# A mixture-of-experts kernel: the second and third expert run in two row tiles of 64, a chunk's two pieces of 272 tokens side by side

## The chip, the cores and the metric

One core of a Trainium2 chip runs the whole program. The metric is the device time of one execution in microseconds, the median over runs. The core has engines that work side by side, each through its own list of instructions in order, and wait for one another by semaphores: TensorE (PE: matrix products into PSUM banks; its loads of the stationary operand are listed as PEld), VectorE (DVE), ScalarE (ACT), GpSimd (POOL) and SyncE (SP, which here issues most of the DMAs).

## The reference

Linear attention (16 heads of 28) and a mixture of 8 experts with two chosen per token run on the same 2048 x 448 input, and a gate per token mixes them. The change is in the experts:

```python
logits = xf @ w_gate
topk_idx = jnp.argsort(-logits, axis=-1)[:, :K]          # K = 2
gates = _softmax(jnp.take_along_axis(logits, topk_idx, axis=-1), axis=-1)
for e in range(E):                                       # E = 8
    mask = (topk_idx == e)
    w = (gates * mask).sum(-1, keepdims=True)
    h = _silu(xf @ w1[e]) @ w2[e]                        # 448 -> 1792 -> 448
    out = out + w * h
...
return g * a + (1 - g) * b
```

## The kernel before

The attention part and the routing come first, and then the experts, ordered by how many tokens chose them, the fullest first. Experts are named 0 to 7 here. Each has room for a fixed number of tokens (`ROOMS`: 552, 544, 544, 504, 504, 504, 496, 488); a loop at the end takes what is above it. The first three (`LARGE` = 3) have more than 512, so `extra(e)` is 40, 32 and 32 tokens; the extras of 32 are called narrow.

Every float32 operand is split into a rounded part (names ending in h) and the rest (names ending in l), and a product is made of three: high by high, high by low, low by high.

**First layer.** The 1792 hidden units of an expert are worked in 14 chunks of 128 (`fc`). For a chunk the weights w1 stand in the array and the tokens stream past. The depth of 448 is three blocks of 128 and one of 64. Experts 0 to 2 use the whole array (`first`, products in `mm3` at L144): the tokens go in two pieces of half the room (276 or 272 columns), one after the other, and a piece takes 11 products: 8 for the high part of the tokens, with the 64 rows that the last block leaves free used for a low part, and 3 for the low part. Experts 3 to 7 use the array as two row tiles of 64 rows (`first_pair`, `in_halves`, L1038): a round is two products of 64 rows that run side by side, one in each half of the array, for two chunks with all tokens (504, 496 or 488 columns). Depth 448 is seven half blocks of 64, three products each: 21 rounds for the two chunks. The first 12 rounds have chunk 0 in the lower half and chunk 1 in the upper, and the last 9 have them the other way round.

**Between the layers.** `gated` takes a sum from its PSUM bank: ACT applies Silu (L1071), DVE makes the high part (a cast, L1077) and the low part (a subtraction, L1080), and for narrow experts copies the extra tokens' columns (L1075). The sums have the two banks "A", used in turn.

**Second layer.** For a chunk, four blocks of 128 tokens (`c` = 0 to 3; `c` = 4 is expert 0's extra tokens) are multiplied with w2 and added up over the 14 chunks: 12 products of 448 columns a chunk, 14 in expert 0. Experts 0 to 2 do it with the whole array (`second`, `share`, L1156), experts 3 to 7 in row tiles for two chunks at a time (`second_pair`, L1122: 24 rounds, blocks 0 and 1 in one half while 2 and 3 are in the other, then exchanged). The narrow extra tokens are multiplied at the end of an expert in `side_by_side` (L1138). Sums of blocks 2 and 3 lie in one double bank, the others in four banks "O". At an expert's end `leave` scales each sum by the token's gate: even blocks by DVE (L1181), odd ones by ACT (L1179), and POOL scatters the rows.

**Order of the work.** The order on each engine is that of the code. A loop over the 112 chunks prepares the next weights (`halve`: ACT copies, DVE subtracts), the next expert's tokens (`gathers` asks for them, `tokens` turns and splits them), and then does its products. For experts 0 to 2 a finished chunk is put into `held`, and its second layer comes one or two chunks later; only expert 2's last two go through the queue. For experts 3 to 7 a generator `queue` runs through second-layer pairs round by round, and `go_on(n)` takes n rounds from it; the pair's first layer is 12 rounds, then 12 of the queue, the other 9, and 12 of the queue. When a bank's sum passes from one half of the array to the other, `meet` places a wait: SP waits for the earlier product, and TensorE waits for SP.

Of the kernel before, what the change touches and what calls it, by code (L numbers as in the profile page):

```python
# [83 lines left out]
SPLITS = {0: (7, 8), 1: (9, 10), 2: (11,), 3: (12,), 4: (13,), 5: (14,), 6: (15,)}  # L84
FILL = ((0, 0), (0, 1))
APART = 24


@with_exitstack
def gated_mix(ctx: ExitStack, tc: tile.TileContext, xt, xq, wk, wq, wv, wphi, wo, w12, out):  # L90
# [15 lines left out]
    def bank(tag, name):  # L106
        pool, n = banks[tag]
        return pool.tile([P, 512], F32, tag=tag, name=name, bufs=n)
# [693 lines left out]
    def extra(e):  # L802
        return EXS[e] if e < LARGE else 0
# [5 lines left out]
    def narrow(e):  # L809
        return 0 < extra(e) <= 32  # L810
# [45 lines left out]
    def tokens(e, c):  # L856
        if c == 0:
            pool = pf if e % 2 else pw
            xg[e] = (pool.tile([P, 4, CAP], F32R, tag="xgh", name=f"xgh{e}", bufs=1),
                     pool.tile([P, 4, MAIN] if e >= LARGE else [P, 3, CAP], F32R, tag="xgl", name=f"xgl{e}", bufs=1))  # L860
        xgh, xgl = xg[e]
        if (e, c) not in xg:
            return
        t = xg[e, c]
        n, m = (4, P) if c < nm else (-(-extra(e) // 32), extra(e))
        xt_ = pm.tile([P, 4, P], F32, tag="xt", name=f"xgt{e}{c}")
        for b in range(n):
            nc.vector.transpose(xt_[:, :, b * 32:(b + 1) * 32], t[:, b].rearrange("p (c k) -> p c k", c=4))
        yield
        m = min(m, ROOMS[e] - c * P)  # L870
        at = slice(c * P, c * P + m)
        both(xgh[:, :, at], xgl[:, :, at], xt_[:, :, 0:m], e >= LARGE)


    def first_tokens(c):
# [147 lines left out]
        beats.append(i)  # L1023
        reached["pe"] = i

    def in_halves(o, xh, xl, wh, wl):
        rounds = []
        for own, turned_ in (((0, 1, 2, 3), False), ((0, 1, 2), True)):
            for s in own:
                for w, x in ((wh, xh), (wl, xh), (wh, xl)):  # L1030
                    one = [(1 - a if turned_ else a, a) for a in range(2)]
                    rounds.append([(i, a, w[half[a], s, i * P:(i + 1) * P], x[half[a], s])
                                   for i, a in (reversed(one) if turned_ else one)])
        for n, one in enumerate(rounds):
            if n == 12:
                yield
            for i, a, l, r in one:
                meet(("first", i), a, lambda: nc.tensor.matmul(o[i], l, r, start=n == 0, stop=n == len(rounds) - 1),  # L1038
                     n == 0)

    def first_pair(e, pair):
        n = ROOMS[e]
        xgh, xgl = (x[:, :, 0:n] for x in xg[e])
        hp = [bank("A", f"hp{e}_{2 * pair + i}")[:, 0:n] for i in range(2)]
        yield from in_halves(hp, xgh, xgl, *wts[e * (NFC // 2) + pair, 1])
        for i in range(2):
            gated(e, 2 * pair + i, 0, hp[i])

    def first(e, fc, hf):
        s, i = divmod(e * NFC + fc, 2)  # L1050
# [34 lines left out]


    def accs(e):
        own = [nm, 0, 1] if extra(e) else [0, 1] if e + 1 < E else range(nm)
        a = {c: bank("O", f"acc{e}{c}") for c in own}
        if e + 1 == E:  # L1090
            return a
        pair = two_banks(f"acc{e}").rearrange("p j n -> p (j n)")
        for i in range(2):
            a[2 + i] = pair[:, i * 512:(i + 1) * 512]
        return a
# [13 lines left out]
    def second_pair(e, pair):  # L1109
# [3 lines left out]
        if narrow(e) and ends:  # L1113
            for at in range(0, NFC, BATCH):
                side_by_side(e, range(at, min(at + BATCH, NFC)))
        todo = [(c, l, r) for c in range(nm) for i in range(2) for l, r in products(e, 2 * pair + i, c)]
        n = len(todo) // 2
        todo = [(a, *one) for k in range(2 * n) for a, one in enumerate((todo[k], todo[k - n]))]
        of = [one[1] for one in todo]
# [4 lines left out]
            if k % 2 and k + 1 < len(todo):  # L1124
                yield
        if ends:
            leave(e, (2, 3, *order(e)[:-2]))
            if e == E - 2:
                settle()
        yield  # L1130
# [66 lines left out]
    def order(e):  # L1197
        return (*([nm] if extra(e) else []), *range(nm))
# [15 lines left out]
    for t in range(NT + 2):  # L1214
# [67 lines left out]
        if SPLIT <= t < SPLIT + 3 and splits:  # L1282
            if next(splits[0], 0) == 0:
                del splits[0]
                if splits:
# [9 lines left out]
    pf = pf_stack.enter_context(tc.tile_pool(name="pf", bufs=2, reuse_waits="tile"))  # L1295
    load(1)
    held = []
    queue = (h for e, pair in [(LARGE - 1, NFC // 2 - 1), *((e, pair) for e in range(LARGE, E)
                               for pair in range((NFC - LATE * (e == E - 1)) // 2))] for h in second_pair(e, pair))

    def go_on(n):
# [4 lines left out]
    for s in range(E * NFC):  # L1306
        e, fc = divmod(s, NFC)
        k, i = divmod(s, 2)
        token = tokens(e + 1, fc - 9) if e + 1 < E and 9 <= fc <= 9 + nm else iter(())
        next(token, 0)  # L1310
        if i == 0 and k + 2 < E * NFC // 2:
            load(k + 2)
# [4 lines left out]
        if e + 1 < E and fc == 4:  # L1317
            asked = gathers(e + 1)
        if e + 1 < E and fc >= 4:
            for _ in range(2):  # L1320
                next(asked, None)
        if e < LARGE:
            for hf in range(2):
                if (e, fc, hf) not in fill:
                    first(e, fc, hf)
            held.append((e, fc))
            advance(1)
            while len(held) > (1 if e == 0 or fc == 0 else 2):
                h = held.pop(0)
                second(*h)  # L1330
                if h[1] == NFC - 1:
                    leave(h[0], order(h[0]))
            continue
        advance(1)
        n = 3 * nm
        if e == E - 1 and fc > NFC - LATE:
            n = n // 2 if fc < NFC - 1 else 0
        if fc % 2 == 0:
            f = first_pair(e, fc // 2)
            next(f)  # L1340
            go_on(n)
            next(f, None)
        else:
            go_on(n)
# [114 lines left out]
```

## Time and profile before

| | |
|---|---|
| time, median of 3 runs | 792.2 us (791.98 to 792.21) |
| the profiled execution | 792.33 us, of which the span from the first to the last instruction is 790.5 us |
| instructions in the profile | 18467 |
| granted TensorE clock, mean | 0.993 of full |
| TensorE products | busy 777.1 us, 98% of the span, 7542 |
| TensorE weight loads | 718.6 us, 91%, 7542 |
| VectorE | 481.6 us, 61% |
| ScalarE | 309.3 us, 39% |
| GpSimd | 336.8 us, 43% |
| DMA | 85.95 MB, 109 GB/s on average |

The profile is one execution, and its times are counted from the start of the span. Products are pipelined, so a row's length is longer than the distance from one start to the next; distances between starts tell how fast TensorE goes on. A wait is put down to the engine or transfer that ended it last; "issue" stands for idle time that ends without anything the profile shows.

### The profile page before, as it was taken

What the parts mean: (1) busy time and instruction counts of PE and PEld (TensorE: products, weight loads), DVE (VectorE), ACT (ScalarE), POOL (GpSimd) and SP (SyncE); (2) the same over time, 40 slices, a digit from 0 to 9 for tenths busy, and PEclk for the clock granted to TensorE, in tenths of its full rate; (3) what the DMA queues carried; (4) which work ended last, traced back from release to release, by engine and by line L of the source; (5) the groups of instructions that cost most, each with busy time, mean ns of one, the idle gap of its engine ahead of it and who ended that gap; (6) DMA issues with size and microseconds to landing.
All of it is one profiled execution on the core that took longest, in us unless ns stands there. A gap on an engine that the chain in (4) does not pass through costs nothing.

```text
span 790.5 us, 18467 instructions
## 1 busy us (share of the span) xinstructions
PE 777.1 (98%) x7542; PEld 718.6 (91%) x7542; DVE 481.6 (61%) x1045; ACT 309.3 (39%) x522; POOL 336.8 (43%) x318
## 2 busy tenths in 40 slices
PE   9999999999999999999999998999999999999995
PEld 6888888888999999998998897999999999999994
DVE  4798978778775865675574543554744555475431
ACT  5543455666533443333242322332433333243221
POOL 5667877875132235414540445144325405423003
PEclk9999999999999999999999998999999999999998
DMA  8420000153433346317541552364345336434403
GB/s 274 126 86 1 2 3 26 34 125 124 140 124 124 118 83 191 102 63 158 146 134 51 126 144 87 107 153 130 122 120 152 134 118 160 140 126 110 137 2 47
DMA packets 39789, 85.95 MB, mean 109 GB/s; under 512 B 11313, under 2 KB 20929, under 8 KB 39701
## 3 DMA queue, kind: packets, MB, share of 16 engines
q1 hardware_dynamic: 29332, 67.88, 26.2%
q0 software_dynamic: 10224, 16.61, 11.3%
q8 instruction: 61, 1.00, 0.6%
q10 hardware_dynamic: 144, 0.23, 0.1%
q14 instruction: 28, 0.22, 0.1%
HBM read 71.89 MB, written 12.82 MB: 107 GB/s over the span
## 4 chain that ended last, share of the span: by engine, by line
PE 84%; issue 10%; DVE 3%; POOL 1%; ACT 1%; POOLq 0%; DVEq 0%; ACTq 0%
PE acc L1122 16%; PE hp L1038 16%; PE hp L144 15%; PE acc L1156 13%; PE ao L144 5%; PE pk L144 4%; PE pq L658 3%; PE pv L144 2%; PE n L909 2%; PE pv L355 2%; PE early L658 1%; PE et L729 1%; PE kv L637 1%; POOL out_dram L994 1%; PE acc L1138 1%
## 5 line engine op out<-in xcount | busy, mean ns | idle before, releaser
L1122 PE MATMUL acc<-w2h,hx 64*128 64x448 f32 (+3 forms) x1088 | 194.3, 366 | 0.1
L828 POOL DMA_INDIRECT xg<-in_xq_dram,idq x114 | 127.4, 1118 | 155.0 <-PE hp L1038 57.1
L1071 ACT ACTIVATE hs<-hp 128x272 f32<-128x272 f32 (+4 forms) x154 | 70.8, 483 | 312.9 <-issue 179.4
L1077 DVE CAST hx<-hs 128x504 fp32r<-128x504 f32 (+5 forms) x154 | 55.6, 361 | 208.0 <-ACT hs L1071 201.0
L1122 PEld LDWEIGHTS acc<-w2h,hx 64*128 64x128 f32 (+3 forms) x1088 | 162.5, 184 | 5.6 <-ACT y L1179 1.6
L1122 PE MATMUL acc<-w2l,hx 64*128 64x448 f32 (+3 forms) x544 | 155.7, 366 | 0.0
L1038 PE MATMUL hp<-xgh,w1h 64*128 64x504 f32 (+2 forms) x490 | 146.3, 387 | 1.2 <-issue 1.2
L1038 PE MATMUL hp<-xgh,w1l 64*128 64x504 f32 (+2 forms) x490 | 145.9, 386 | 0.6 <-issue 0.6
L1038 PE MATMUL hp<-xgl,w1h 64*128 64x504 f32 (+2 forms) x490 | 145.6, 385 | 0.9 <-issue 0.9
L994 POOL DMA_INDIRECT out_dram<-y,tabm x32 | 52.2, 1631 | 172.4 <-DVE y L1181 164.0
L1156 PE MATMUL acc<-w2h,hx 128*128 128x448 f32 (+2 forms) x366 | 111.7, 365 | 0.0
L1122 PEld LDWEIGHTS acc<-w2l,hx 64*128 64x128 f32 (+3 forms) x544 | 97.7, 184 | 1.4
L1038 PEld LDWEIGHTS hp<-xgh,w1h 64*128 64x128 f32 x490 | 88.0, 185 | 5.5 <-issue 2.8
L1038 PEld LDWEIGHTS hp<-xgh,w1l 64*128 64x128 f32 x490 | 87.9, 185 | 4.0 <-issue 1.2
L1038 PEld LDWEIGHTS hp<-xgl,w1h 64*128 64x128 f32 x490 | 88.0, 185 | 3.2 <-issue 0.5
L1080 DVE TENSOR_TENSOR hx<-hs,hx 128x276 fp32r<-128x276 f32 (+5 forms) x168 | 84.9, 512 | 5.3
L144 PE MATMUL hp<-xgh,w1h 128*128 128x272 f32 (+1 forms) x336 | 87.9, 289 | 0.0
L144 PE MATMUL hp<-xgh,w1l 128*128 128x272 f32 (+1 forms) x336 | 87.8, 289 | 0.0
L797 DVE TENSOR_TENSOR w1l<-wr,w1h 128x1024 fp32r<-128x1024 f32 x56 | 68.2, 1219 | 11.1 <-ACT w1h L795 9.9
L1156 PEld LDWEIGHTS acc<-w2h,hx 128*128 128x128 f32 (+2 forms) x366 | 68.0, 186 | 6.2 <-issue 0.7
L1156 PE MATMUL acc<-w2l,hx 128*128 128x448 f32 (+2 forms) x190 | 69.4, 365 | 0.0
L144 PEld LDWEIGHTS hp<-xgh,w1l 128*128 128x128 f32 x336 | 63.2, 188 | 0.6
(236 smaller groups left out, 1393.5 us busy)
## 6 DMA issues: line engine op xcount, KB each, us to landing
wr<-in_w_dram SPq DMA_DIRECT2D x56, 512.0 KB
wr<-in_w_dram SPq DMA_DIRECT2D x46, 448.0 KB
kept<-in_w_dram SPq DMA_DIRECT2D x10, 448.0 KB
out_dram<-aos SPq DMA_DIRECT2D x16, 224.0 KB
xr<-in_xt_dram SPq DMA_DIRECT2D x10, 256.0 KB
xg<-in_xq_dram,idq POOLq DMA_INDIRECT x114
xr<-in_xt_dram SPq DMA_DIRECT2D x6, 192.0 KB
out_dram<-zero SPq DMA_DIRECT2D x5, 224.0 KB
```

The source lines that it names most:

```text
L144: reached["pe"] = nc.tensor.matmul(o, a, b, start=i == 0, stop=i == n - 1)
L355: nc.tensor.matmul(pv2[t][:, 0:VG], a, (WL if k == "w" else WH)["v"][:, c], start=c == 0 and k == "h", stop=c == 3 and k == "w")
L658: nc.tensor.matmul(pq[t].rearrange("p h d -> p (h d)"), x, w, start=k == 0, stop=k == 10)
L797: nc.vector.tensor_tensor(out=l, in0=raws[s][layer - 1], in1=h.bitcast(F32), op=ALU.subtract)
L828: i = nc.gpsimd.indirect_dma_start(out=t[:, b], out_offset=None, in_=xq, in_offset=bass.IndirectOffsetOnAxis(ap=idq[:, e, 4 * c + b:4 * c ...
L994: return nc.gpsimd.indirect_dma_start(out=out, out_offset=bass.IndirectOffsetOnAxis(ap=idx_ap, axis=0), in_=y, in_offset=None, compute_op= ...
L1038: meet(("first", i), a, lambda: nc.tensor.matmul(o[i], l, r, start=n == 0, stop=n == len(rounds) - 1), n == 0)
L1071: nc.scalar.activation(hs[:, tsl], hp, AF.Silu)
L1077: nc.vector.tensor_copy(h[:, tsl], hs[:, tsl])
L1080: nc.vector.tensor_tensor(out=h[:, a + o:b + o], in0=hs[:, a:b], in1=h[:, a:b].bitcast(F32), op=ALU.subtract)
L1122: meet((e, c), a, lambda: nc.tensor.matmul(acc[e][c][:l.shape[1], 0:D], l[half[a]], r[half[a]], start=new, stop=ends and c not in of[k + 1 ...
L1156: i = nc.tensor.matmul(acc[e][c][:l.shape[1], 0:D], l, r, start=fc == 0 and k == 0, stop=fc == NFC - 1 and k == len(pr) - 1)
```

## The change

Experts 1 and 2 now run in row tiles too (`TILED` = 1 is the first expert that does). A round holds the same chunk for both pieces of 272 tokens, one piece in each half of the array (`first_pieces`), so a chunk takes 21 rounds of 272 columns in place of 22 products. Its rounds are 12, then `LEAD` = 5 rounds of the queue, the other 9, and the remaining 7 of the queue; in the first two chunks of expert 1 the queue gets 7 and 7, since expert 0's last pair has 28 rounds. The second layer of experts 1 and 2, and of expert 0's last two chunks, goes through `second_pair`.

Beside it: tokens of experts 1 and 2 are split into a full low part (a depth of four blocks, as in experts 3 to 7); those of expert 1 are asked for three at a time rather than two, and are turned one chunk earlier; the sums' banks are handed out in another order (`accs`), and two experts leave in another order (expert 0: blocks 4, 2, 3, 0, 1; expert 1: 2, 3, 4, 0, 1; both had 4, 0, 1, 2, 3).

```diff
+TILED = 1
+LEAD = 5
...
-    def in_halves(o, xh, xl, wh, wl):
+    def in_halves(o, ops):
         rounds = []
         for own, turned_ in (((0, 1, 2, 3), False), ((0, 1, 2), True)):
             for s in own:
-                for w, x in ((wh, xh), (wl, xh), (wh, xl)):
+                for w, x in ((2, 0), (3, 0), (2, 1)):
                     one = [(1 - a if turned_ else a, a) for a in range(2)]
-                    rounds.append([(i, a, w[half[a], s, i * P:(i + 1) * P], x[half[a], s])
+                    rounds.append([(i, a, ops[i][w][half[a], s], ops[i][x][half[a], s])
                                    for i, a in (reversed(one) if turned_ else one)])
...
+    def first_pieces(e, fc):
+        s, i = divmod(e * NFC + fc, 2)
+        w = [x[:, :, i * P:(i + 1) * P] for x in wts[s, 1]]
+        n = ROOMS[e] // 2
+        hp = [bank("A", f"hp{e}_{fc}_{hf}")[:, 0:n] for hf in range(2)]
+        yield from in_halves(hp, [(*(x[:, :, hf * n:(hf + 1) * n] for x in xg[e]), *w) for hf in range(2)])
+        for hf in range(2):
+            gated(e, fc, hf, hp[hf])
...
-        own = [nm, 0, 1] if extra(e) else [0, 1] if e + 1 < E else range(nm)
+        own = [nm, 0, 1] if e < TILED else [0, 1, nm] if extra(e) else [0, 1] if e + 1 < E else range(nm)
...
-            leave(e, (2, 3, *order(e)[:-2]))
+            leave(e, (*order(e)[-2:], *order(e)[:-2]) if e else (nm, 2, 3, 0, 1))
...
-    queue = (h for e, pair in [(LARGE - 1, NFC // 2 - 1), *((e, pair) for e in range(LARGE, E)
+    queue = (h for e, pair in [(TILED - 1, NFC // 2 - 1), *((e, pair) for e in range(TILED, E)
...
-        token = tokens(e + 1, fc - 9) if e + 1 < E and 9 <= fc <= 9 + nm else iter(())
+        at = fc - (9 if e else 8)
+        token = tokens(e + 1, at) if e + 1 < E and 0 <= at <= nm else iter(())
...
-            for _ in range(2):
+            for _ in range(2 if e else 3):
                 next(asked, None)
-        if e < LARGE:
+        if e < TILED:
...
-            while len(held) > (1 if e == 0 or fc == 0 else 2):
+            while len(held) > (1 if fc < NFC - 1 else 2):
...
-        if fc % 2 == 0:
+        if extra(e):
+            a, b = (7, 7) if (e, fc) in ((1, 0), (1, 1)) else (LEAD, n - LEAD)
+            f = first_pieces(e, fc)
+            next(f)
+            go_on(a)
+            next(f, None)
+            go_on(b)
+        elif fc % 2 == 0:
```

Three places of the order show what moves. The first is TensorE at the passage from expert 0 to expert 1 (`hp_13_1` is the second piece of expert 0's last chunk, `acc` the second layer's sums, `hp_0_0` and `hp_0_1` the pieces of expert 1's first chunk). Before, with the waits of each row in brackets, the middle products left out:

```order
L144 MATMUL hp_13_1_4426<-xgl_2995,w1h_4207 128x276 x3
L1156 MATMUL acc_3617<-w2h_4273,hx_12_4363 80x448 [waits DVE_49]
L1156 MATMUL acc_3617<-w2l_4274,hx_12_4363 80x448
L1156 MATMUL acc_3618<-w2h_4273,hx_12_4363 128x448
...
L1156 MATMUL acc_3620<-w2l_4274,hx_12_4363 128x448
L1156 MATMUL acc_3620<-w2h_4273,hx_12_4363 128x448
L144 MATMUL hp_0_0_4466<-xgh_4058,w1h_4341 128x272 [waits Activation_49]
```

Now, in the same place:

```order
L146 MATMUL hp_13_1_4421<-xgl_2995,w1h_4220 128x276 x3
L1040 MATMUL hp_0_0_4447<-xgh_4002,w1h_4344 128x272 [waits Activation_49]
L1040 MATMUL hp_0_1_4448<-xgh_4002,w1h_4344 128x272 [waits Activation_49]
L1040 MATMUL hp_0_0_4447<-xgh_4002,w1l_4345 128x272 [waits DVE_49]
L1040 MATMUL hp_0_1_4448<-xgh_4002,w1l_4345 128x272
L1040 MATMUL hp_0_0_4447<-xgl_4003,w1h_4344 128x272
```

The 14 second-layer products of chunk 12 that stood between the two experts have moved behind expert 1's first rounds, and both pieces of its first chunk begin together. The second place is DVE at expert 0's leaving, which now stands in expert 1's second chunk (`hx_1` is that chunk's split, `y_4622`, `y_4626` and `y_4632` are blocks 4, 2 and 0 of expert 0):

```order
L1092 TENSOR_TENSOR hx_1_4598<-hs_1_4597,hx_1_4598 128x272 [waits DVE_49]
L1087 COPY hxe_1_4599<-hs_1_4597 128x32 [waits Activation_49]
L1089 CAST hx_1_4598<-hs_1_4597 128x240
L1092 TENSOR_TENSOR hx_1_4598<-hs_1_4597,hx_1_4598 128x240 [waits DVE_49]
L1194 TENSOR_SCALAR y_4622<-acc_3617,tabx 80x448 [waits PE_49]
L1194 TENSOR_SCALAR y_4626<-acc_3620,tabm 128x448 [waits PE_49]
L1194 TENSOR_SCALAR y_4632<-acc_3618,tabm 128x448
L799 TENSOR_TENSOR w1l_4643<-wr_9_4439,w1h_4642 128x1024 [waits DMAHW0_49,Activation_49]
```

Before, these three stood in the order 4, 0, 2 behind the split of expert 1's first chunk; now block 2 comes ahead of 0, and all are a chunk later. The third place is TensorE in expert 1's third chunk, with the first second-layer products of that expert (`acc_4675` is the double bank of blocks 2 and 3, `acc_4672` the bank of block 0):

```order
L1040 MATMUL hp_2_0_4646<-xgl_4003,w1h_4443 128x272
L1040 MATMUL hp_2_1_4647<-xgl_4003,w1h_4443 128x272
L1135 MATMUL acc_4672<-w2h_4400,hx_0_4508 128x448 [waits DVE_49]
L1135 MATMUL acc_4675<-w2h_4400,hx_0_4508 128x448 [waits Activation_49]
L1135 MATMUL acc_4672<-w2l_4401,hx_0_4508 128x448
...
L1135 MATMUL acc_4675<-w2l_4401,hx_1_4598 128x448
L1040 MATMUL hp_2_0_4646<-xgh_4002,w1h_4443 128x272 [waits SP_sequencer_49]
L1040 MATMUL hp_2_1_4647<-xgh_4002,w1h_4443 128x272 [waits SP_sequencer_49]
```

The chunk's first 12 rounds, five rounds of the second layer, and then the exchange of halves with its wait through SP; the double bank waits for ACT.

More of the change, by code (lines that the diff above doesn't have):

```diff
@@ L859, in tokens @@
             xg[e] = (pool.tile([P, 4, CAP], F32R, tag="xgh", name=f"xgh{e}", bufs=1),
-                     pool.tile([P, 4, MAIN] if e >= LARGE else [P, 3, CAP], F32R, tag="xgl", name=f"xgl{e}", bufs=1))
+                     pool.tile([P, 4, MAIN if e >= LARGE else CAP] if e >= TILED else [P, 3, CAP], F32R, tag="xgl", name=f"xgl{e}", bufs=1))
         xgh, xgl = xg[e]
@@ L871, in tokens @@
         at = slice(c * P, c * P + m)
-        both(xgh[:, :, at], xgl[:, :, at], xt_[:, :, 0:m], e >= LARGE)
+        both(xgh[:, :, at], xgl[:, :, at], xt_[:, :, 0:m], e >= TILED)
     def first_tokens(c):
@@ L1044, in first_pair @@
         hp = [bank("A", f"hp{e}_{2 * pair + i}")[:, 0:n] for i in range(2)]
-        yield from in_halves(hp, xgh, xgl, *wts[e * (NFC // 2) + pair, 1])
+        yield from in_halves(hp, [(xgh, xgl, *(w[:, :, i * P:(i + 1) * P] for w in wts[e * (NFC // 2) + pair, 1]))
+                                  for i in range(2)])
         for i in range(2):
             gated(e, 2 * pair + i, 0, hp[i])
+    def first_pieces(e, fc):
[6 more added lines that the diff above has]
+            gated(e, fc, hf, hp[hf])
     def first(e, fc, hf):
@@ L1115, in second_pair @@
                 side_by_side(e, range(at, min(at + BATCH, NFC)))
-        todo = [(c, l, r) for c in range(nm) for i in range(2) for l, r in products(e, 2 * pair + i, c)]
+        todo = [(c, l, r) for c in (range(nm) if narrow(e) else order(e)) for i in range(2)
+                for l, r in products(e, 2 * pair + i, c)]
         n = len(todo) // 2
```

## Prediction

> **What bounds it now.** I read the page first (the chain that ended last), then who TensorE waited for, then TensorE by stage.
>
> ```profile
> PE 84%; issue 10%; DVE 3%; POOL 1%; ACT 1%; POOLq 0%; DVEq 0%; ACTq 0%
> ```
> ```profile
> PE hp L1038 <- issue: 2.7, 5, 0.9
> PE warm L241 <- DVE blank L239: 1.1, 1, 1.1
> PE n L909 <- issue: 0.6, 2, 0.4
> PE n L909 <- DVE w L925: 0.5, 1, 0.5
> ```
> ```profile
> 203.00:279.00 76.00, 76.00 (x488) 72.63 (x487) 54.21 (x165) 28.56 (x50) 18.17 (x18) 1.00 0.38 125
> 279.00:356.00 77.00, 77.00 (x509) 74.38 (x508) 49.41 (x124) 29.46 (x53) 30.44 (x23) 1.00 0.41 113
> 356.00:429.00 73.00, 73.00 (x488) 68.16 (x488) 43.86 (x105) 26.87 (x47) 30.10 (x24) 1.00 0.48 132
> ```
> The chain is TensorE; in all 790 us it waits for another engine only at the start and once for 0.5 us (columns: total, times, longest). The windows are roughly experts 0, 1 and 2 (length, then busy time of PE, weight loads, DVE, ACT, POOL): PE is busy throughout, DVE under 72%. So time here is the sum of products times their spacing, and an edit counts if it changes that sum or opens a hole in it.
>
> The spacing is read from the timeline (start, length, engine, line, names, forms, count), by starts: 12 second-layer products of expert 1 and the 22 first-layer ones of expert 2's first chunk; and, in two row tiles, 9 rounds of expert 3's first layer and 12 of its second.
>
> ```profile
> 350.56 0.36 PE L1156 MATMUL acc<-w2h,hx 128*128 128x448 f32 x1
> 352.99 0.29 PE L144 MATMUL hp<-xgh,w1h 128*128 128x272 f32 x1
> 355.75 0.36 PE L1156 MATMUL acc<-w2h,hx 128*128 128x448 f32 x1
> ```
> ```profile
> 502.08 0.56 PE L1038 MATMUL hp<-xgh,w1h 64*128 64x504 f32 x2
> 504.12 0.54 PE L1122 MATMUL acc<-w2h,hx 64*128 64x448 f32 x2
> 506.55 0.58 PE L1038 MATMUL hp<-xgh,w1h 64*128 64x504 f32 x2
> ```
> Full array: 12 products of 448 columns take 352.99 - 350.56 = 2.43, 0.2025 each; 22 of 272 take 355.75 - 352.99 = 2.76, 0.1255 each. Row tiles: 9 rounds of 504 take 2.04, 0.2267 each; 12 rounds of 448 take 2.43, 0.2025 each. The line through the two full-array points (0.0770 for 176 columns) gives 0.2270 at 504. A round of two half-height products costs what one full product of its columns costs.
>
> **The sum.** First layer: a chunk goes from 22 products to 21 rounds of 272 columns. I price the round by that line, 0.1255. Per chunk 22 x 0.1255 - 21 x 0.1255 = 0.1255; 28 chunks: **-3.5**. Second layer: 12 rounds of 0.2025 for 12 products, nothing. Expert 0's last two chunks become 28 rounds for 28 products, nothing. The narrow products of the last rows stay as they are.
>
> A round of 272 is not in this trace, and it needs two weight loads in 0.1255. Transposes of the attention part (timeline) and the page's row of expert 3's loads bound their cost:
>
> ```profile
> 170.38 0.71 PE L729 MATMUL et<-ident,eq 64*128 64x64 f32 x16
> 170.93 0.41 PE L948 MATMUL ot<-ident,om 64*128 64x64 f32 x8
> ```
> ```profile
> L1038 PEld LDWEIGHTS hp<-xgh,w1h 64*128 64x128 f32 x490 | 88.0, 185 | 5.5 <-issue 2.8
> ```
> 16 products with 16 loads of 64x128 start within 0.55: two loads and two products in 0.069, so a round of 0.1255 has room. The other end is two of the 0.185 loads one after the other, 0.37 a round, +144 over 588 rounds; the rows of 0.069 exclude it, and I take zero. [...]
>
> Instructions double in this stage: 4 in 0.1255, 32 per us, in bursts of 12 rounds, 26 over a chunk. The densest 20 us of the attention part:
>
> ```profile
> 169.00:189.00 20.00, 20.00 (x455) 17.56 (x456) 16.07 (x38) 14.51 (x25) 15.66 (x16) 1.00 0.65 193
> ```
> Here 911 were issued in 20 us, 46 per us: no cost.
>
> **New holes.** Both pieces' sums now end together, and banks are freed later or asked for sooner. Latencies come from a chunk of expert 1, in the timelines of PE (its last first-layer product starts at 308.69 + 2 x 0.1255 = 308.94), ACT and DVE:
>
> ```profile
> 308.69 0.54 PE L144 MATMUL hp<-xgl,w1h 128*128 128x272 f32 x3
> ```
> ```profile
> 307.94 0.40 ACT L1071 ACTIVATE hs<-hp 128x272 f32<-128x272 f32 x1 [2.60 <-issue]
> 309.27 0.40 ACT L1071 ACTIVATE hs<-hp 128x272 f32<-128x272 f32 x1 [0.93 <-PE hp L144]
> 309.56 1.05 ACT L795 ACTIVATE w1h<-wr 128x1024 fp32r<-128x1024 f32 x1
> ```
> ```profile
> 308.37 0.30 DVE L1077 CAST hx<-hs 128x272 fp32r<-128x272 f32 x1 [1.91 <-ACT hs L1071]
> 308.71 0.44 DVE L1080 TENSOR_TENSOR hx<-hs,hx 128x272 fp32r<-128x272 f32 x1
> 309.70 0.18 DVE L1075 COPY hxe<-hs 128x32 f32<-128x32 f32 x1 [0.55 <-ACT hs L1071]
> 309.79 0.28 DVE L1077 CAST hx<-hs 128x240 fp32r<-128x240 f32 x1
> 310.11 0.41 DVE L1080 TENSOR_TENSOR hx<-hs,hx 128x240 fp32r<-128x240 f32 x1
> ```
> And from expert 3's leaving, with expert 4's first second-layer products behind it: timelines of DVE, ACT and PE, the groups of the two y's (count, busy, mean ns) in experts 1 and 2, and the weight loads' waits.
>
> ```profile
> 517.97 1.27 DVE L1181 TENSOR_SCALAR y<-acc,tabm 128x448 f32<-128x448 f32 x2
> ```
> ```profile
> 518.68 1.16 ACT L1179 ACTIVATE y<-acc,tabm 120x448 f32<-120x448 f32 x2 [2.53 <-DVE y L1181]
> ```
> ```profile
> 518.96 0.88 PE L1122 MATMUL acc<-w2h,hx 64*128 64x448 f32 x2
> 519.37 0.67 PE L1122 MATMUL acc<-w2l,hx 64*128 64x448 f32 x2
> ```
> ```profile
> L1181 DVE TENSOR_SCALAR y<-acc,tabm 128x448 f32<-128x448 f32 x4 | 2.7, 681 | 1.6 <-PE acc L1156 1.5
> L1179 ACT ACTIVATE y<-acc,tabm 128x448 f32<-128x448 f32 x4 | 2.5, 634 | 10.0 <-PE acc L1156 7.4 <-DVE y L1181 1.3 <-issue 1.3
> ```
> ```profile
> PEld acc L1122 <- ACT y L1179: 1.6, 4, 0.5
> ```
> With T the start of a chunk's last round: Silu at T+0.33, the second 0.29 later and done at T+1.02; cast 0.43 after its Silu, subtraction 0.34 after, 0.44 long, copy, cast 0.09 later, subtraction 0.32 later, 0.41 long: DVE is through with both pieces at T+2.36. At the change from expert 3 to 4, the first second-layer product into the double bank waits for ACT's y, which waits for DVE's y (0.68 long, the next 1.27 - 0.68 = 0.59 later), which stands in DVE's queue; TensorE starts 0.06 after ACT's y (518.68 + 0.63 = 519.31, then 519.37). It loses 0.4 there, four times 1.6 in all, with 12 rounds of 504 (2.72) as cover.
>
> Hole 1, expert 0 to 1. Leaving is queued on DVE behind chunk (1, 1)'s split: y of the extra rows at T+2.36, y of token block 2 0.59 later, 0.68 long, ACT's y of block 3 0.63 long, 0.06: T+4.3. TensorE gets there at T + 0.13 + 7 x 0.2025 + 12 x 0.1255 = T+3.05. **+1.25**. Queued behind the waiting product is all of TensorE.
> Hole 2, expert 1 to 2: the same without the extra rows' y ahead, 0.6 less: **+0.65**.
> Hole 3, start of expert 1: its first round needs both banks of first-layer sums, and nothing stands between it and expert 0's last product any more (second-layer products of 2.8 us did). Silu ends at T+0.73, 0.06, against T+0.13: **+0.65**.
> Bounds for each: nothing below; 0.4 more if the tiles' halves lie 0.4 apart, as expert 3's starts do.
>
> At nothing: chunk to chunk inside an expert, banks are free at T+1.02+0.06, TensorE asks at T+0.13+1.42 = T+1.55 (cover: 7 second-layer rounds; without it 0.95 a chunk). Splits are ready at T+2.36, asked for from T+3.05 (three rounds later for the new chunk). The change of halves after round 12 waits through SP for round 12's product: 0.33 to notice and 0.06 to release, by the rows above, against 5 rounds, 1.14; SP's weight loads stand behind these waits, as in the last five experts, where TensorE's list of waits shows none for a weight. Tokens of expert 1 come one chunk earlier on DVE, which is 71% busy in that window, and change DVE's two subtractions for one. The change of tile mode moves from expert 3 to 1.
>
> Sum: -3.5 + 1.25 + 0.65 + 0.65 = -0.95. The profiled execution's own time is 792.33 (span 790.5 and 1.8 around it), so 791.4; the median of the runs is 0.13 lower, so **791.3**.
>
> **Rivals.** (a) *No holes*: if the splits of chunk (1, 1) run behind the leaving, or halves keep apart so that covers hold, -3.5: 788.8. Against: DVE takes its queue in order.
> (b) *Slower: ACT becomes late in every chunk.* ACT has a weight copy (1.05) or token copy in each chunk beside the two Silus. If one is running when the sums end, the first Silu starts up to 1.05 late, and 0.47 is the slack (1.55 - 1.08): 0.1 to 0.6 lost in each chunk hit. At 0.2 in 28 chunks: +5.6, 797. Against: a copy follows the previous Silu at once (309.56), and is done 3 us before the next.
> (c) *The unexplained stop.* TensorE nearly stops once, released by nothing that the profile shows:
>
> ```profile
> 471.00:481.50 10.50, 10.50 (x102) 10.50 (x100) 5.52 (x10) 2.50 (x4) 8.19 (x8) 1.00 0.54 178
> 481.50:492.50 11.00, 8.31 (x42) 6.29 (x40) 4.62 (x11) 2.21 (x3) 4.74 (x5) 0.69 0.16 47
> 492.50:502.00 9.50, 9.50 (x90) 9.05 (x90) 6.38 (x16) 4.10 (x6) 2.07 (x2) 0.99 0.36 119
> ```
> 42 products at 9.6 per us are 4.4 us of work in 11: 6.6 lost, partly at a granted clock of 0.69 in that window. The change puts some 2000 more instructions on TensorE ahead of it. If the stop goes: 784.7; if a second comes: 798. The agreeing run times (791.98 to 792.33) say that it belongs to this program; I let it stay.
> (d) *The change doesn't do what it says*: the halves don't run side by side at this length, a round takes 2 x 0.1255, +70, 862. Against: the 0.2267 of 504.
> (e) *Loads in turn*: two loads that follow each other outlast the products, a round takes up to the 0.37 of the rows, +144, 936. Against: 0.069. [...]
>
> **Numbers.** Forecast 0.52 (790.0 to 793.0), (a) 0.12 (788.3 to 790), (b) 0.13 (793 to 799), (c) gone 0.10, a second 0.08, (d) 0.02, (e) 0.01, others 0.02. The range takes in the forecast, (a), most of (b) and part of a second stop: 788.3 to 797. A measurement tells 0.2% (1.6 us) from no change: faster is (a), a stop gone and a little of the forecast's edge, 0.28; slower (b), a second stop, (d), (e), 0.23; within, 0.49.
>
> **What would show it.** Starts of first-layer rounds in experts 1 and 2 0.1255 apart, a chunk in 5.07 instead of 5.19; waits of TensorE or its loads on ACT's y of 1.25 and 0.65 at the third chunk of experts 1 and 2, and on ACT's Silu of 0.65 at expert 1's start. Wrong if Silu is waited for in every chunk, if a round takes more than 0.13, or if the stop at 481 has gone or come twice.

## The result, and the profile after

| | before | after |
|---|---|---|
| time, median of 6 runs each | 792.09 us (790.51 to 792.44) | 801.12 us (799.76 to 802.94) |
| ratio | | 1.0118, 95% interval 1.0106 to 1.013 |
| profiled execution | 792.33 us, span 790.5 | 800.86 us, span 799.1 |
| TensorE products | 777.1 us, 98%, 7542 | 777.5 us, 97%, 8442 |
| granted clock, mean | 0.993 | 0.991 |

One run of the kernel before, in comparison 5 below, took 942.9 us at a granted clock of 0.752 and stands in no ratio.

Slower by 9.0 us, and outside the range of the prediction. The chain of waits of the changed kernel has almost the same shares as before (issue 10%, TensorE 83% instead of 84%), so it doesn't tell where the time went:

```profile
PE 83%; issue 10%; DVE 2%; DMA 1%; ACT 1%; another core or an unknown queue 1%; POOL 1%; SPq 0%; POOLq 0%; DVEq 0%; ACTq 0%
```

Where it went is read by comparing one landmark in both traces. The first product of 504 columns (the start of expert 3) stands in the timelines of TensorE of before, then of after:

```profile
428.83 0.49 PE L1038 MATMUL hp<-xgh,w1h 64*128 64x504 f32 x2
```
```profile
438.81 0.46 PE L1040 MATMUL hp<-xgh,w1h 64*128 64x504 f32 x2
```

Experts 1 and 2 end 9.98 us later, where the forecast had 0.95 earlier. The rest of the program, from there to the end of the span, is 1.4 us shorter (799.1 - 438.81 = 360.3 against 361.7). So the loss lies in the two changed experts. The lists of waits of that stretch of after (278 to 450 us; total, times, longest), the weight loads first, then the products:

```profile
PEld hp L1040 <- SPq L1017: 9.5, 10, 7.0
PEld acc L1151 <- issue: 3.3, 13, 0.4
...
PEld hp L1040 <- ACT hs L1083: 0.4, 1, 0.4
```
```profile
PE hp L1040 <- SPq L1017: 6.6, 1, 6.6
```

TensorE waits for SP, at the change of halves, which the forecast had at nothing: once for 6.6 us, and nine times for 2.5 together (9.5 - 7.0). By stretches (busy time and instructions of TensorE's products, its loads, DVE, ACT, GpSimd; then granted clock, DMA share, GB/s), after:

```profile
356.00:396.00 40.00, 39.76 (x509) 37.08 (x508) 20.02 (x46) 12.16 (x23) 15.87 (x10) 1.00 0.48 117
396.00:413.00 17.00, 10.42 (x108) 9.92 (x107) 4.22 (x13) 3.15 (x6) 8.30 (x9) 0.80 0.30 94
413.00:429.00 16.00, 16.00 (x204) 15.25 (x203) 11.03 (x32) 6.52 (x12) 7.10 (x6) 1.00 0.35 110
...
486.00:502.00 16.00, 13.04 (x99) 11.42 (x97) 7.01 (x16) 4.12 (x6) 8.77 (x10) 0.89 0.32 103
```

There are two stops now. The one that was there before is still in expert 3 (486 to 502), and a second has come in expert 2, with the clock halved behind it: 6.6 us of wait, 2.5 of shorter waits and the forecast's -0.95 make 8.2 of the 9.98. The 1.8 left is about what half clock costs there: from the restart at 408.4 to 412.3 the granted clock is 0.50, so 3.9 us of work run at half speed and lose 1.9. The second stop in the timelines of after, TensorE's products, SP's issues and GpSimd:

```profile
400.34 0.28 PE L1040 MATMUL hp<-xgl,w1h 64*128 64x272 f32 x1
...
401.45 0.39 PE L1135 MATMUL acc<-w2l,hx 64*128 64x448 f32 x2
408.42 0.66 PE L1040 MATMUL hp<-xgh,w1h 64*128 64x272 f32 x2 [6.58 <-SPq L1017]
408.81 0.50 PE L1040 MATMUL hp<-xgh,w1l 64*128 64x272 f32 x2
409.04 0.50 PE L1040 MATMUL hp<-xgl,w1h 64*128 64x272 f32 x2
```
```profile
396.56 0.33 SPq L774 DMA_DIRECT2D kept<-in_w_dram  x1
416.10 0.45 SPq L774 DMA_DIRECT2D wr<-in_w_dram  x2
```
```profile
387.75 1.32 POOL L996 DMA_INDIRECT out_dram<-y,tabx  x1 [2.00 <-DMA out_dram<-y,tabx]
391.84 1.32 POOL L996 DMA_INDIRECT out_dram<-y,tabx  x1 [2.77 <-DMA out_dram<-y,tabx]
393.46 1.02 POOL L830 DMA_INDIRECT xg<-in_xq_dram,idq  x1 [0.30 <-issue]
394.79 1.76 POOL L830 DMA_INDIRECT xg<-in_xq_dram,idq  x1 [0.30 <-issue]
...
405.79 0.94 POOL L830 DMA_INDIRECT xg<-in_xq_dram,idq  x1 [0.30 <-issue]
```

SP has no weight load to issue between 396.9 and 416.1, so nothing stands in front of its wait. What it waits for, the last product of round 12, started at 400.34; and SP's list of waits puts an 8.0 us wait there down to "remote", an end that no recorded event explains:

```profile
SPq L1017 <- remote: 8.0, 1, 8.0
```

What runs through the stop is GpSimd: the row gathers for expert 3, ten in a train with no pause over 0.3, from 393.46 to 406.7; TensorE goes on 1.7 us after its end. (The expectations below count only the part of a train at an even pitch, as eight or nine.) In before, the stop of expert 3 has the same picture: a train of twelve from 468.75 to 485.1, TensorE slow from 481.7 to 486.7.

```profile
468.75 1.01 POOL L828 DMA_INDIRECT xg<-in_xq_dram,idq  x1 [0.30 <-PE hp L1038]
...
484.14 0.95 POOL L828 DMA_INDIRECT xg<-in_xq_dram,idq  x1 [0.30 <-issue]
```

The trains are there because GpSimd comes free late: it issues the scatter-adds of the expert that left, and of the four of its shared rows each after the first waits for the landing of the one before (4.00, 2.00 and 2.77 us; the last two are the `tabx` rows above). The gathers, due two a chunk, are then overdue and follow each other. Trains were to be tested, against two rivals: SP's queue, and a stop that belongs to a count of TensorE's instructions (9,800 or so in before's trace, 9,900 in after's, 11,600 for the second).

### The profile page after: what moved, and what is told of

It reads as the page before. It is cut to its first block, busy times and chain, and to the rows that moved or that the text cites. A ratio compares the mean times of both kernels' runs of the same rounds, so it can differ in the third digit from the quotient of the medians.

```text
span 799.1 us, 20349 instructions
## 1 busy us (share of the span) xinstructions
PE 777.5 (97%) x8442; PEld 722.8 (90%) x8442; DVE 475.8 (60%) x1035; ACT 306.5 (38%) x522; POOL 338.0 (42%) x318
## 4 chain that ended last, share of the span: by engine, by line
PE 83%; issue 10%; DVE 2%; DMA 1%; ACT 1%; another core or an unknown queue 1%; POOL 1%; SPq 0%; POOLq 0%; DVEq 0%; ACTq 0%
PE hp L1040 25%; PE acc L1135 25%; PE hp L146 5%; PE pk L146 5%; PE acc L1169 4%; PE ao L146 4%; PE pq L660 3%; PE pv L146 3%; PE n L911 2%; PE pv L357 2%; PE early L660 1%; PE kv L639 1%; DMA out_dram<-aos 1%; POOL out_dram L996 1%
## 5 line engine op out<-in xcount | busy, mean ns | idle before, releaser
L1135 PE MATMUL acc<-w2h,hx 64*128 64x448 f32 (+4 forms) x1540 | 272.9, 365 | 1.3 <-issue 0.9
L1040 PE MATMUL hp<-xgh,w1h 64*128 64x272 f32 (+3 forms) x882 | 219.1, 344 | 7.7 <-SPq L1017 6.6
L1135 PEld LDWEIGHTS acc<-w2h,hx 64*128 64x128 f32 (+4 forms) x1540 | 215.6, 184 | 7.7 <-ACT y L1192 2.2
L1040 PE MATMUL hp<-xgl,w1h 64*128 64x272 f32 (+3 forms) x882 | 217.1, 341 | 1.9 <-issue 1.9
L1040 PE MATMUL hp<-xgh,w1l 64*128 64x272 f32 (+3 forms) x882 | 217.5, 342 | 0.1
L1135 PE MATMUL acc<-w2l,hx 64*128 64x448 f32 (+4 forms) x772 | 207.9, 365 | 0.0
L1040 PEld LDWEIGHTS hp<-xgh,w1h 64*128 64x128 f32 x882 | 143.6, 185 | 15.2 <-SPq L1017 9.5
L1135 PEld LDWEIGHTS acc<-w2l,hx 64*128 64x128 f32 (+4 forms) x772 | 128.8, 184 | 1.3
L797 ACT ACTIVATE w1h<-wr 128x1024 fp32r<-128x1024 f32 x56 | 59.2, 1057 | 0.0
L1169 PE MATMUL acc<-w2h,hx 128*128 128x448 f32 (+2 forms) x140 | 42.9, 366 | 0.0
```

The costliest lines, as they stand in the source:

```text
L797: nc.scalar.activation(h, raws[s][layer - 1], AF.Copy)
L1135: meet((e, c), a, lambda: nc.tensor.matmul(acc[e][c][:l.shape[1], 0:D], l[half[a]], r[half[a]], start=new, stop=ends and c not in of[k + 1 ...
L1169: i = nc.tensor.matmul(acc[e][c][:l.shape[1], 0:D], l, r, start=fc == 0 and k == 0, stop=fc == NFC - 1 and k == len(pr) - 1)
```

## Experiments

Kernels of one comparison ran on one chip, beside the same runs of the kernel before. The kernel before falls into two groups by comparison, not by run, and this turned out to be the key:

| comparison | before, median (lowest to highest, runs) | changed kernels, median in us (ratio, 95% interval) |
|---|---|---|
| 1 | 792.09 (790.5 to 792.4, 6) | the change 801.12 (1.0106 to 1.013) |
| 2 | 791.32 (789.6 to 793.7, 25) | a_pace2 794.11 (1.0022 to 1.0053), a_pace23 793.70 (1.0018 to 1.0049), b_pace3 790.79 (0.9978 to 1.0005), a_bunch4 808.50 (1.0185 to 1.0239) |
| 3 | 785.21 (784.3 to 785.9, 17) | a_pace23b 788.44 (1.0026 to 1.006), a_pace23b_lead6 787.49 (1.002 to 1.0043), b_pace3b 789.52 (1.003 to 1.0059), b_bunch2 784.92 (0.9987 to 1.0006) |
| 4 | 792.18 (789.8 to 793.9, 13) | after_again 805.19 (1.0123 to 1.0187), a_weave 789.23 (0.9957 to 0.998), b_weave 785.58 (0.9903 to 0.994), a_weave_lead6 786.24 (0.9916 to 0.9956) |
| 5 | 785.21 (784.2 to 786.4, 30; one more at 942.9) | a_bunch2 783.65 (0.9972 to 0.9991), b_bunch2_again 785.06 (0.9992 to 1.0012), a_weave_mid 784.24 (0.9984 to 1.0003), b_weave_again 785.05 (0.9988 to 1.0007) |
| 6 | 784.88 (784.0 to 785.7, 19) | after_third 783.87 (0.9971 to 0.999), b_bunch2_third 785.65 (1.0003 to 1.0022) |

Names with a_ start from the changed kernel, names with b_ from the kernel before.

**Breaking the trains, and making one.** a_pace2 starts expert 2's gathers in chunk 7, three a chunk; a_pace23 also those of expert 3 in chunk 6; b_pace3 does only the latter, on the kernel before.

```diff
-        if e + 1 < E and fc == 4:
+        begin = {2: 7}.get(e, 4)
+        if e + 1 < E and fc == begin:
             asked = gathers(e + 1)
-        if e + 1 < E and fc >= 4:
-            for _ in range(2 if e else 3):
+        if e + 1 < E and fc >= begin:
+            for _ in range((3 if fc < begin + 4 else 4) if begin > 4 else 2 if e else 3):
```

`{2: 7, 3: 6}` in a_pace23, `{3: 6}` in b_pace3. a_bunch4 does the opposite where there was no stop:

```diff
+        begin = 7 if e == 4 else 4
...
+            for _ in range((10 if fc == begin else 2) if e == 4 else 2 if e else 3):
```

> The changed kernel; GpSimd's 16 row gathers that are issued in expert 2 (for expert 3) start in chunk 7 and go out three a chunk (four in the last), instead of two a chunk from chunk 4, where they pile up behind the scatter-adds of expert 1 and then run as one train of eight (396.9 to 406.7). Theory G (a train of gathers that does not pause, beside row-tiled products, holds TensorE until 1.6 us after its last one): the stop at 401.5 and the half clock behind it go, 6.8 + about 3 us, so 791 to 792; the stop of expert 3 stays. Theory S (SyncE's queue: the wait for the change of halves stands behind weight loads): the gathers are nothing to it, 801. Theory N (TensorE stops after a certain number of instructions, here near its 9,900th, for their delivery): 801, with the stop at the same count.

> As a_pace2, and the 16 gathers issued in expert 3 (for expert 4) start in chunk 6 and go out three a chunk. G: both stops go, the second with 5.0 of crawl and about 1.6 of half clock: 784.5 to 786, faster than both kernels. S and N: 801, or 795 if only the crawl has to do with gathers.

> The kernel before the change; only the 16 gathers issued in expert 3 start in chunk 6 and go out three a chunk. G: its single stop (481.7 to 486.7, then half clock, 6.6 us in all) goes: 785.5. N: the stop stays where it is, near TensorE's 9,750th instruction: 792. S says nothing of this stop: 792.

> The changed kernel; in expert 4, which has no stop, ten of the 16 gathers for expert 5 are issued together in chunk 7 and the rest two a chunk. G: a third stop comes in expert 4, which starts 4 to 6 us into the train (about 12 us long) and ends 1.6 us after the train, so 5 to 8 us and half clock behind it: 807 to 813. S and N: no new stop, 801.

a_pace2 took 794.1: the stop of expert 2 is gone from its profile, that of expert 3 is not.

```profile
396.00:413.00 17.00, 16.89 (x207) 15.46 (x206) 10.76 (x28) 6.13 (x12) 10.45 (x10) 1.00 0.43 148
471.00:491.00 20.00, 16.94 (x138) 15.60 (x136) 10.40 (x21) 5.46 (x8) 14.09 (x13) 0.91 0.39 130
```

Its profiled run, 791.3, is as expected, but the runs scatter up to 797.8, and the median is 2 to 3 above the expectation; no trace shows what makes the others longer. a_bunch4 took 808.5, as expected: in its expert 4, where the changed kernel's TensorE is busy all the time, a third stop has come (the same stretch, the changed kernel first, then a_bunch4):

```profile
556.00:577.00 21.00, 21.00 (x198) 19.35 (x196) 12.90 (x29) 7.59 (x11) 8.34 (x8) 1.00 0.37 121
```
```profile
556.00:577.00 21.00, 17.27 (x117) 13.64 (x116) 7.63 (x17) 4.24 (x6) 13.04 (x14) 0.85 0.29 91
```

117 products instead of 198. It begins later than expected, about 12 us into a train of 14 gathers (551.8 to 570.5), and ends 1.6 us behind it. Neither SP's queue nor a count of instructions changes there; both rivals fall (a_pace2, too, runs past the count of 9,900 without a stop). a_pace23 and b_pace3 missed: 793.7 and 790.8, because GpSimd is still at its scatter-adds in chunk 6 of expert 3 (the last begins at 467.16 in b_pace3), and the gathers again went out as a train of twelve (b_pace3, GpSimd):

```profile
468.79 1.08 POOL L828 DMA_INDIRECT xg<-in_xq_dram,idq  x1 [0.30 <-PE hp L1038]
...
483.85 0.94 POOL L828 DMA_INDIRECT xg<-in_xq_dram,idq  x1 [0.30 <-issue]
```

**A longer pause, and a control without row tiles.** In a_pace23b and b_pace3b expert 3's gathers start in chunk 8 and the token steps come a chunk later; a_pace23b_lead6 has one round more of cover; b_bunch2 sends twelve gathers together in chunk 7 of expert 2 of the kernel before, which is not row-tiled.

```diff
-        at = fc - (9 if e else 8)
+        at = fc - (10 if e == 3 else 9 if e else 8)
...
-LEAD = 5
+LEAD = 6
```

> The changed kernel with the gathers issued in expert 2 as in a_pace2, and those issued in expert 3 started in chunk 8, three a chunk, with the four token steps of expert 4 a chunk later (chunks 10 to 13); a_pace23 did not break the train of expert 3 (nine gathers, 476.1 to 487.3), since GpSimd came free only in chunk 8. Theory G (trains): no train of over four, no crawl in expert 3: 6 us below a_pace2's profiled 791.3, 785 to 788, and runs closer together than a_pace2's 791.3 to 797.8. Theory N (a count of instructions): a stop near TensorE's 9,900th instruction or in expert 3 all the same, 793.

> As a_pace23b, with six instead of five second-layer rounds between a chunk's first 12 rounds and its turned nine. Theory H (in the ten or so chunks beside gathers the word of round 12 reaches TensorE through SyncE 0.1 to 0.3 late, since the gathers delay it): one round of 0.2 more of cover takes most of it, 1.5 to 2.5 less than a_pace23b. Rival: the waits are the gathers' own slowing of TensorE, wherever it stands: no change (within 0.5).

> The kernel before the change, with the gathers issued in expert 3 started in chunk 8, three a chunk, and the token steps of expert 4 a chunk later. G: its single stop goes, 785 to 786.5, 0.993. N: stays, 791.3.

> The kernel before the change, where expert 2 is not row-tiled; twelve of the 16 gathers for expert 3 are issued together in chunk 7 of expert 2, a train of some 15 us beside full-height products. If a train stops TensorE only beside row tiles (32 instructions a us on TensorE at 272 columns, 17.5 at 504, against 17 untiled here): 791 to 792, no new stop. If a train of that length stops TensorE whatever it runs: a new stop 6 to 8 us into the train until 1.6 us after it, some 8 us and half clock, 800 to 804.

Here the kernel before itself took 785.2, as without its stop, and nothing was left to remove: b_pace3b at 789.5 only shows what later token steps cost (a hole of 2.3 at the start of expert 4; the mean granted clock of its profiled run was 0.995, b_bunch2's 0.997). b_bunch2 ran unharmed, but in a comparison in which no train harms, so it tells nothing of row tiles. a_pace23b_lead6's one us less than a_pace23b has overlapping runs (786.5 to 788.4 and 787.8 to 789.7) and no waits for SP to explain it; it settles nothing.

**Weaving, with the change once more.** The last three scatter-adds of the shared rows go between the gathers of the next expert, so that GpSimd never falls behind:

```diff
+WOVEN = (1, 2)
...
+            for k, (v, ids) in enumerate(todo):
+                if c == nm and e in WOVEN and k:
+                    late.append(functools.partial(add, v, ids))
+                else:
+                    add(v, ids)
...
             for _ in range(2 if e else 3):
                 next(asked, None)
+            if late:
+                late.pop(0)()
```

> The changed kernel as it is, once more, beside the kernel before: in the last comparison the kernel before took 785.2 us, with a train of eleven gathers and no stop in expert 3, where it took 792.1 and 791.3 in the others. If the stops belong to where a program runs as well as to its trains, both kernels lose them together here: before 785, this 784 to 787, a ratio of 0.999 to 1.003. Otherwise as in the first comparison: 792 and 801, the ratio 1.012.

> The changed kernel; the last three of the four scatter-adds of the shared rows of experts 1 and 2, each of which waits 2 to 5 us for the one before it, go between the gathers of the next expert, one a chunk, so that the gathers start in chunk 4 and go out two a chunk. No train, and no token step moved. Theory G: no stop in experts 2 and 3 wherever it runs: 784 to 788. If trains have nothing to do with it: as after_again.

> The kernel before the change with the same woven order. G: no stop: 784.5 to 786.5; the change itself is then a_weave less this: by the prediction's sum -1, and with the late words of round 12 (some ten of 0.2 to 0.3) +1 to +2.

> a_weave with six second-layer rounds instead of five between the first 12 rounds and the turned nine. If the late word of round 12 costs 2 to 3 us in experts 1 and 2: 1 to 2 less than a_weave. If it is the gathers' slowing of TensorE itself: the same within 0.5.

In this comparison the stops were there: before 792.2, the change 805.2. Without trains before loses 6.6 (785.6) and the change 16.0 (789.2). The stretch of before's stop, in b_weave, is full, 106 products against 42:

```profile
481.50:492.50 11.00, 11.00 (x106) 11.00 (x104) 8.27 (x20) 4.40 (x7) 5.21 (x5) 1.00 0.46 160
```

What is left of the change is +3.65 (789.23 - 785.58), and its weight loads still wait for SP, for 3.7 in all (a_weave, then a_weave_lead6, same list):

```profile
PEld hp L1043 <- SPq L1020: 3.7, 10, 1.0
...
PEld hp L1043 <- ACT hs L1086: 1.3, 2, 0.9
```
```profile
PEld acc L1154 <- issue: 3.3, 13, 0.4
PEld acc L1138 <- ACT y L1195: 2.2, 3, 1.2
PEld acc L1138 <- issue: 0.7, 2, 0.4
PEld hp L1043 <- ACT hs L1086: 0.6, 2, 0.4
```

With six rounds of cover no wait for SP is left and 3.0 us go (786.24). So the ten late words cost most of these 3 us (in the same two lists the waits for Silu also fall, from 1.3 to 0.6), and 0.7 is left of the change. One of them in a_weave, TensorE and GpSimd:

```profile
408.02 0.33 PE L1043 MATMUL hp<-xgl,w1h 64*128 64x272 f32 x2
408.15 0.41 PE L1138 MATMUL acc<-w2h,hx 64*128 64x448 f32 x2
...
409.29 0.46 PE L1043 MATMUL hp<-xgh,w1h 64*128 64x272 f32 x2
```
```profile
407.15 1.06 POOL L832 DMA_INDIRECT xg<-in_xq_dram,idq  x1 [3.70 <-PE hp L1043]
408.52 1.47 POOL L832 DMA_INDIRECT xg<-in_xq_dram,idq  x1 [0.30 <-issue]
```

Round 12 starts at 408.02, and the turned round, which needs its word, at 409.29, 1.27 later, beside a pair of gathers; the cover is 1.14 (0.13 and five rounds of 0.2025). The stop itself is 0.13, and the restart, two rounds 0.23 apart, costs another 0.1; nine like it and one of 1.0 make the 3.

**What remains without either.** a_weave_mid writes a pair of gathers behind a chunk's last turned round (`step()` after `next(f, None)`), so that it no longer lies across round 12; a_bunch2 and b_bunch2_again send the twelve gathers together, with and without row tiles; after_third is the change itself, b_bunch2_third the control again.

```diff
+        begin = 7 if e == 2 else 4
...
+            for _ in range((12 if fc == begin else 2) if e == 2 else 2 if e else 3):
```
```diff
+        if e not in (1, 2):
+            step()
...
             next(f, None)
+            step()
             go_on(b)
```

The first is a_bunch2's (and, with 2 for all other experts, b_bunch2's); in the second, a_weave_mid's, `step()` issues the gathers and the woven scatter-add of a chunk.

> The changed kernel (expert 2 row-tiled) with twelve of the 16 gathers for expert 3 issued together in chunk 7 of expert 2, a train of about 15 us. G: a stop of TensorE in expert 2, longer than the changed kernel's own since the train is: 803 to 812 where the kernel before takes 791 to 792; no stop where that takes 785. If trains have nothing to do with it: as the changed kernel.

> The kernel before the change (expert 2 not row-tiled) with the same twelve gathers together. If a train stops TensorE only beside row tiles: as the kernel before, within 1 us, whatever a_bunch2 does. If beside any products: 8 to 15 us more than the kernel before.

> a_weave, with the gathers that are issued in experts 1 and 2 written behind a chunk's last turned round instead of ahead of the chunk, so that a pair runs in the 3 us between that round and the next chunk's round 12, no longer across round 12; five rounds of cover as in the change. If the gathers delay the words: the ten waits go without more cover, 785.5 to 786.5 (a_weave took 789.2, with six rounds of cover 786.2). If five rounds are too little by themselves: 789. If the delay moves to the word that releases Silu: 787 to 788, with TensorE waiting for Silu.

> b_weave once more, as the measure for a_weave_mid on the same chip: 785.6. By the prediction's sum for the change without late words and a second stop, a_weave_mid is then 1 below it, 784.6.

> The changed kernel as it is. Where the kernel before takes 785.2: no stop, no late words, so the prediction's sum alone: 783.5 to 785, a ratio of 0.998 to 1.000. Where the kernel before takes 791 to 792: 800 to 806, as twice already.

> The kernel before the change with twelve of the 16 gathers issued in expert 2 sent together in its chunk 7, beside products of full height. Where the kernel before takes 791 to 792: the same within 1 if a train stops TensorE only beside row tiles, 800 to 807 if beside any products. Where it takes 785.2: the same within 0.5, which tells nothing new.

Comparisons 5 and 6 both had the kernel before at 785. There the change itself is faster: after_third 783.87 against 784.88, 0.9981 (0.9971 to 0.999), 1.0 us. Its trace has even longer trains (16 gathers from 394.35 to 417.2, 14 up to 486.1) and no stop, and no wait for SP at all in the list of its two experts:

```profile
PEld acc L1151 <- issue: 3.3, 13, 0.4
PEld acc L1135 <- ACT y L1192: 2.0, 3, 1.2
PEld acc L1135 <- issue: 0.7, 2, 0.4
PEld hp L1040 <- ACT hs L1083: 0.4, 1, 0.4
```
```profile
396.00:413.00 17.00, 17.00 (x225) 16.63 (x223) 12.09 (x33) 7.54 (x14) 13.34 (x13) 1.00 0.46 156
```

Pairs of gathers lie across its round 12 as in a_weave (307.82 and 309.28 around one at 308.6), yet nothing waits. So both losses need what made comparisons 1, 2 and 4 differ, and by the records that isn't the chip: those of comparisons 2 and 6 give the same chip number, 14. "Where a program runs", as after_again's expectation has it, doesn't separate the two groups, as far as that number tells.

One thing does tell them apart: how many semaphore updates the recording caught. The ten kept traces of comparisons 1, 2 and 4 hold 7,081 to 7,250 of them, the ten of comparisons 3, 5 and 6 hold 8,751 to 8,925. The changed kernel as it is has 20,349 instructions in all three of its traces, but 7,116 and 7,139 updates in after and after_again against 8,901 in after_third; of those that tell of landed DMAs, 4,475 in after, a quarter is missing. The recording lost records in every trace of the comparisons with stops, also where no stop was left (a_weave 7,081, b_weave 7,127). Whether the loss of records and the stops have one cause isn't shown.

a_bunch2's train is as harmless here (783.65); a_weave_mid against b_weave_again gives the change -0.8; that it also cures the late words where they occur isn't shown, since none occurred. The control without row tiles never met a comparison with stops. The nearest thing to it is b_pace3's expert 2, not row-tiled, in comparison 2: GpSimd sends ten gathers there from 383.96 to 398.7, with one pause of 0.6, and TensorE loses nothing (the list of its waits is empty from 384 to 400),

```profile
386.00:400.00 14.00, 14.00 (x95) 13.57 (x94) 7.56 (x16) 4.06 (x8) 9.95 (x9) 1.00 0.41 123
```

while in a_pace23, same comparison, row-tiled, six gathers (399.62 to 407.85) cost a hole of 2.0. That points to row tiles, whose rounds of 272 columns need 32 instructions a us of TensorE (4 in 0.1255) against 16 (2 in 0.1255) for untiled products at the same pitch, without settling it.

## Why the prediction was wrong

- **Rounds, loads, tiles: right.** Rounds start 0.1255 apart as forecast: in after_third the twelfth round of two chunks in a row starts at 318.72 and 323.79, 5.07 apart, the forecast's chunk.

```profile
318.72 0.29 PE L1040 MATMUL hp<-xgl,w1h 64*128 64x272 f32 x1
...
323.79 0.29 PE L1040 MATMUL hp<-xgl,w1h 64*128 64x272 f32 x1
```

The weight loads cost nothing: two of them one after the other, 0.185 each in after as in before, would have made a round 0.37, which the chunk of 5.07 excludes. Rivals (d) and (e) fall.

- **Holes: right in place, nearly in size.** Waits for ACT's y of 1.2 at expert 1's third chunk (forecast 1.25) and 0.6 at expert 2's (0.65; the third of the list, 0.3, is the passage to expert 3, there before too). Waits for Silu at expert 1's start 0.4 (0.65). Rival (a), no holes, falls.
- **The sum: right where nothing else happens.** -0.95 forecast, -1.0 in comparison 6. From the first product of expert 0 to the first of expert 3 after_third takes 226.04 (201.23 to 427.27) and b_bunch2_third, of the same comparison, 227.55 (200.99 to 428.54): -1.5, so beside the saving of 3.5 the holes came to 2.0 in place of 2.55.
- **"The change of halves after round 12 waits through SP ... at nothing": this step failed, in the comparisons with stops.** The price itself, 0.33 to notice and 0.06 to release, was read from ACT, not from SP, but it holds in after_third: round 12's products start at 318.72 and 318.89, and SP's two instructions that wait for them stand 0.3 to 0.4 later. In a_weave's example they come 1.2 after the round's start at 408.02, and the turned round 1.27 after it, against 1.14 of cover; so the word is late before it reaches SP (SP's rows in after_third, 318.7 to 319.4, then in a_weave, 407.5 to 411):

```profile
L1017 SPq EVENT_SEMAPHORE  x2: 17/17/17, 319.1 to 319.2; - x2
```
```profile
L1020 SPq EVENT_SEMAPHORE  x2: 17/17/17, 409.2 to 409.3; - x2
```

Nine or ten such chunks cost 2.5 (after) to 3.0 (a_weave against a_weave_lead6). Weight loads ahead of the wait, which the step looked at, had no part in it.
- **Rival (c), "I let it stay", failed as a reading.** The stop was taken as something of this program with no cause to be found, a second as an accident of 0.08, at 6.6. One of its conditions stood in the profile: in GpSimd's row, a train of gathers through the whole of it, which ended 1.6 before the stop did; without it, in b_weave, the kernel before took 6.6 less. The other, what sets comparisons 1, 2 and 4 apart, no trace of before alone could show. The change brought row tiles to expert 2, which had a train already (eight gathers from 385.08 to 396.3, and no stop, in before); a second stop was then to be reckoned with for a reason, not as an accident, though that it takes row tiles isn't settled. Priced, it is 6.6 of wait and 1.8 of half clock. With it and the late words the forecast's own terms give 791.3 + 6.6 + 1.8 + 2.5 - 1.4 (the first stop and the half clock behind it became shorter) = 800.8; measured 801.1. Since 1.8 was the rest of the 9.98, and 1.4 was read from the same two traces, this sum confirms nothing by itself; what stands apart from it is the 1.9 read from the clock.
- **Rival (b), Silu late in each chunk, fell:** one or two waits for Silu in 28 chunks, in the lists shown.

The range failed because it joined the two losses nowhere: the late words alone lie at 794, the second stop alone at 798, the two together at 801.

Of the versions tried, a_weave_lead6 beats both kernels where stops occur (786.2 against 792.2 and 805.2), and so does b_weave, the kernel before without its train (785.6, intervals overlapping). Where none occur the change as it is does as well as any, 783.9.

## What to carry over

A stall with no releaser is to be laid beside every other engine's timeline, not only beside the waits: here the engine that ran through it, and whose train of transfers ended 1.6 us before it, was GpSimd. Before a stage gets more and shorter instructions (32 a us in place of 16 here, though that their number mattered isn't settled), look for such a train in that stage, and see why the engine fell behind; spreading its work is cheaper than the stall (b_weave took 6.6 less than before where the stop occurs, and b_weave_again the same as before where none does). A wait that goes over a third engine should be covered for the worst notice time in the trace, taken beside transfers (1.2 us in a_weave's example, where after_third had 0.3 to 0.4), and a small effect should be measured in more than one comparison: here the sign of the change depended on it. Where two recordings of one program hold different numbers of records (here 7,116 and 8,901 updates), don't take them as made under the same conditions.

## What the hardware showed unexpectedly

- Row gathers of GpSimd following each other at 1.25 us stopped or slowed TensorE in three of six comparisons (1, 2 and 4), until 1.6 to 1.7 us after the last one (before, the change, a_bunch4; 0.6 in a_pace2's expert 3 and 0.1 in a_pace23's expert 2). The stop began 6.3 and 8.4 us into the train beside rounds of 272 columns (a_pace23, the change), about 12 and 13 us beside rounds of 504 (a_bunch4, before). In the other three comparisons trains of 14 and 16 did nothing. Within a comparison the runs of the kernel before agree (789.6 to 793.9 in comparisons 1, 2 and 4; 784.0 to 786.4, and one at 942.9, in the others); one chip number stands in both groups. What sets the groups apart is open, but for the fifth of the semaphore updates that the traces of 1, 2 and 4 lack.
- In the comparisons with stops the word from TensorE over SP also came late beside a pair of gathers: 1.27 us in a_weave's example, 1.2 of it until SP, where SP in after_third needs 0.3 to 0.4.
- Whether this needs the recording is open too: every run here was recorded, and a wait that no recorded event ends (8.0 us of SP in after) can be one whose record is missing (7,116 updates in after, 8,901 in after_third). That the recording also held TensorE back, no run here shows.
- After the 6.6 us stop TensorE went on at half the granted clock (0.50 from 408.4 to 412.3 in after), rounds 0.23 apart in place of 0.1255, and lost about 1.8 us more.
